# Values by key range and a larger weight pool in an attention and mixture-of-experts kernel

## The chip, the cores and the metric

The program runs on one core of a Trainium2 chip. The metric is device time in microseconds of one execution; the kernel before was run three times. Besides, one execution was taken by the hardware profiler; all rows come from that one.

## What is computed

The inputs are q, k, v of 4 batches, 8 heads, 576 positions and 64 dimensions in float32. Two attentions are added: one over queries, keys and values averaged over groups of 4 positions (144 of them), whose result is repeated 4 times, and one over the 576 positions in which a query sees only keys nearer than 4 positions. The sum is laid out as 2304 tokens of 512 numbers. A router takes, from the token times `w_gate` plus noise scaled by a second product, the two best of 8 experts. Each chosen expert computes `relu(x @ w1[e]) @ w2[e]` with 1024 hidden numbers, and the two results are added with softmax weights.

```
out_d = sm_attn(q_d, k_d, v_d)              # means over 4 positions
out_up = np.repeat(out_d, 4, axis=2)
mask = np.abs(pos[:, None] - pos[None, :]) < 4
out_local = np.matmul(softmax(where(mask, scores, -1e9)), v)
x = (out_up + out_local)                    # 2304 x 512
noisy_logits = x @ w_gate + log1p(exp(x @ w_noise)) * noise
out[mask] += top2_w * (relu(x[mask] @ w1[e]) @ w2[e])
```

## The kernel before, in words

**Attention and routing.** The local attention is cut into 20 tiles n, five for each batch, of 116 queries in two halves s of 58; a half sees a window of 64 keys (`geo`, line 661). For each tile the values of both windows are loaded (`l_load_v`, 666), the scores are made in pieces of 32 queries and 38 keys (`l_qk`, 682) on top of a mask that is put there by a product with the identity (687), then maximum, exponential, sum and scaling (`l_max`, `l_exp`, `l_sum`, `l_norm`), a transpose (`l_pt`, 726), the products with the values (`l_pv`, 737), the sum with the pooled attention into `xT` (`l_x`, 761), a transpose to rows (`l_xt`, `l_xtc`) and a store to DRAM (`l_store`, 785), and the router's logits (`l_lg`, `l_lgt`, `l_ls`). Five groups of token tiles are routed (`r_...`), and each token is scattered into a list of its expert by POOL (`r_put`, 950).

In the kernel before, a value tile has for each s two half-tiles of 64 partitions, one for each parity j of the head, with head parity and key range changing places between the two s (`j ^ s`); that makes four transfers of 64 KB, each with 64 x 4 runs of 256 bytes. The scores follow the same order: the PSUM bank is `j ^ s`, and a group of 32 partitions t stands for s = t % 2.

**Who orders the work.** Up to expert 1's first products all work is a list of steps (`Step`, 273), each with an engine, an estimated time, a priority, what it must come after, and the buffers it takes and uses. `run_steps` (309) goes through them in three stages and writes the instructions out: of the steps that an engine could do, it takes the one with the earliest possible start, then the lowest priority number. The resulting order is fixed in the program; the engines run it in order and wait for one another by semaphores. To each priority is added an offset from the table `OFF` (364), four numbers for each kind of step, for the four quarters of its steps. For SP the planner holds a running end of the transfers (`free["move"]`) and lets SP be at most 4 us ahead of it (`LEAD`). `light` steps need not be done at the end of stage 2; they may be taken later. `keep_warm` (431) writes fillers (products of ones, line 440) into holes of PE that it foresees, and where it counts too little work on PE; `LOAD` (464) says how many columns each kind counts for.

**Queues.** All plain loads and stores are issued by SP in the planned order: `t_load` (492, q and k), `vd_load` (549), `l_load_v` (673, with small transfers at 680 for the two tiles at the edges), `l_store` (786), the weights (`fetch_w`, 226 and 229), and six fills of the output with zeros (201, 768 KB each). POOL issues the indirect transfers: lists, gathers of tokens, reads and writes of output rows.

**Expert 0 and the others.** Stages 2 and 3 hold expert 0 (`b_gemm`, 1247, in two parts; `o_part`, 1362) and what prepares expert 1. Each weight tile of 256 KB is fetched into a `raw` buffer of the pool `stage` (three buffers), and split into two parts by ACT (236) and DVE (241). At the end of stage 2 the attention's memory is given back, and the pools for w2, gathered tokens and output rows are opened in its place. Then comes a loop over experts 1 to 7 (1621): for each of 8 column blocks f `gemm1` (1411), for each of 5 token tiles `gemm2` (1442); a fetch is written two blocks ahead of its split.

Of the kernel before, what the change touches and what calls it, by code (L numbers as in the profile page):

```python
# [22 lines left out]
def kernel(  # L23
# [113 lines left out]
    def c_masks():  # L137
        for mi in range(3):
# [73 lines left out]
    raws = {}  # L212
# [60 lines left out]
    class Step:  # L273
        def __init__(self, kind, eng, dur, fn, after=(), new=(), use=(), prio=0.0, move=0.0, light=False, lag=0.0, cols=0, stage=1, table=None):
# [34 lines left out]
    def run_steps(stage):  # L309
# [55 lines left out]
        "a_acc": (-35.8, -29.9, -41.4, 31.4), "a_count": (2.1, 21.3, 57.6, 27.6),  # L365
        "a_holes": (-13.6, -13.6, -13.6, 5.5), "a_list": (-28.2, -28.2, -28.2, -28.2),
        "a_part": (34.5, 17.5, 19.9, 17.3), "a_rows": (63.6, 53.8, 45.5, 68.8), "b_gather": (70, 40.2, 38.5, 70),
        "b_gemm": (70, 70, -1.7, 69.5), "b_hi": (-5.8, -53.4, -5.8, -11), "b_list": (3, -7.6, 32.7, 10.7),
        "b_lo": (-18.8, 26.1, 33.4, 15.7), "b_order": (-3.1, 15.9, 0.8, -53.3), "b_pe": (-23.6, 17.4, 36.4, -2.4),
        "b_relu": (-8.2, 29.4, 20.6, 20.6), "b_rest": (-44.2, -1.4, 0.1, -5), "b_rows": (-15.8, -15.8, -15.8, -15.8),  # L370
        "b_weights": (67.8, 27.4, 37.6, 70), "c_count": (-7.2, 26.4, -2.5, 24.3),
        "c_fills": (-49.8, -50.9, -49.8, -49.8), "c_first": (58.9, 58.9, 58.9, 58.9),
        "c_ids": (-24.5, -3.7, -53.2, -26), "c_masks": (-32.2, -32.2, -32.2, -32.7),
        "c_rank": (43.6, -14.4, 44.9, -11.3), "c_route": (37.4, 35.5, 35.5, 35.5), "c_sel": (36.1, 36.1, 36.1, 36.1),
        "c_tiles": (64.7, -32.5, 60.3, -8.6), "d_exp": (-34.8, -4.1, 50, 48.6), "d_max": (-33.9, -40.6, -31.6, -12.5),
        "d_norm": (-2.9, -28.4, 23.9, -56.6), "d_pt": (7.3, -56.4, -42.1, -22.2), "d_ptc": (53.7, -56.9, -48.7, 21.1),
        "d_pv": (-41, -62.6, -1.1, -6.4), "d_qk": (-38.9, -36.4, -70, 7.8), "d_rz": (-28.1, 38.2, 2.2, 41.2),
        "d_up": (-16.3, 11.3, 13, 23.2), "e_go": (33.5, 40.3, 40.2, 40.3), "e_hi": (13.3, 13.3, 13.3, 11.3),
        "e_lo": (70, 43.8, 66, 70), "e_order": (-0.7, 38.7, 6.6, 25.9), "e_pe": (13.8, 52.4, 45.7, 34.4),
        "fetch_e": (55.6, 41.4, 55.6, 44.5), "fetch_w1": (56.2, 21.6, 43.6, 70), "fetch_w2": (7, 7, 7, 7),  # L380
        "fill_list": (-63.8, -37.3, 46.9, -59.5), "fill_out": (69, 56.5, 66.7, 66.7),
        "gather": (68.9, -37.6, 13.3, 46.3), "hi_e": (45.6, 48.8, -6.3, 59.6), "identb": (64.2, 70, 60.7, 39.3),
        "l_exp": (47.9, 57.6, 9, 32.8), "l_lg": (5, 4, -47.3, -36.8), "l_lgc": (-23, -22.4, 11.2, 3.9),
        "l_lgt": (-19.5, -3.7, 52.2, 58.9), "l_load_v": (-1.4, 7, 18.4, 15.9), "l_ls": (-27.7, -44.1, -11.5, 61.4),
        "l_max": (42, 35.3, -9.2, 40.9), "l_norm": (-40.5, -35.4, -39.8, -38.5),
        "l_norml": (-28.7, -52.7, -53.5, -56.9), "l_pt": (2.8, 3.6, 6.5, -5.2), "l_ptc": (-3.1, 46.3, -56.1, 39.2),
        "l_pv": (12.7, -7.4, 25.3, 7.1), "l_qk": (68.4, 62.8, 45.1, 68.4), "l_store": (-51, -50.8, -23.1, -40.9),
        "l_sum": (52.7, 48.4, 66.6, 66.5), "l_x": (-43.4, -61.4, -62.6, -66.4), "l_xt": (-68.7, -18.3, -5.3, 8.4),
        "l_xtc": (49.6, 19.4, 69.8, 18.1), "list_rows": (-21.4, -21.4, -21.4, -21.4), "lo_e": (31.8, 67.7, 52.9, 47.2),
        "load_list": (50.6, 43.3, 49.1, 57.3), "load_noise": (13.3, 57, 8, 70), "load_wgn": (-25.5, -1, -51.2, 68.7),  # L390
        "masks": (-19.2, -13.1, -19.2, -19.2), "o_mul": (-28.1, -27.4, 34.8, -31.1), "o_part": (-16, 42.8, 37.7, 40.1),
        "o_put": (32.9, 5.5, -9.1, 5.5), "ones": (35.8, -24.2, -12.1, -57), "r_count": (65.3, 69.7, 61.2, 69.7),
        "r_hot": (54.2, 26.5, 59.7, 49.5), "r_oh": (-55.9, 24.4, -20.9, -53.4), "r_pay": (70, 1.5, 69.4, 68.8),
        "r_pos": (70, 70, 70, 50.3), "r_put": (-5.2, -13.1, -12.5, 9.1), "r_slot": (-28.8, 13.6, 60.5, 29.8),
        "r_soft": (-60.1, -60.1, -62.8, -60.1), "r_top": (31.8, -0.7, -39.8, 16.5), "r_wexp": (41.8, 56.1, 54.8, 52.9),
        "r_where": (9.4, 3.3, 5, -29.5), "sp_zero": (47.1, 47.1, 49, 47.4), "split_hi1": (14.2, 5.5, 32.8, 14.2),
        "split_hi2": (46.9, 12.2, 20.3, 25.2), "split_lo1": (46.2, 0.6, 70, 70),
        "split_lo2": (34.7, 30.6, -36.3, 22.4), "t_copy": (58.7, 39.5, -16.7, 23.1),
        "t_load": (-32.5, -18, -20.5, -13.1), "t_new": (-32.4, -69.4, -37.9, 23.9), "t_pe": (-39.8, 51.4, 54.6, 67.6),
        "t_sum": (-57.2, -29.3, -19, -19), "t_sumq": (40.8, 45, 34.7, 48.9), "vd_load": (-1.5, -3.6, -1.9, 9.1),  # L400
        "vd_sum": (-27.8, -4.2, -3.3, -4.2), "vd_sum2": (70, 70, 69.8, 70), "vd_zero": (-70, -44.5, -48.7, 55.6),
        "warm": (-18.5, -7.9, 20, -7.4), "which": (65.1, 66, 60.4, 65.1)}
# [9 lines left out]
    def buf(name, early=False):  # L412
        return Buf(R[name], early or name in EARLY)
# [17 lines left out]
    def keep_warm(t, t1):  # L431
# [23 lines left out]
        while t1 > 8.0 and sum(w for e, w in warm[-64:] if e > t1 - WARM_T) < WARM_C:  # L455
# [8 lines left out]
    LOAD = {"t_pe": 1024, "l_qk": 1536, "l_pt": 1024, "l_pv": 512, "l_xt": 1024, "l_lg": 512, "l_ls": 64, "d_qk": 576,  # L464
            "d_pt": 1024, "d_pv": 864, "b_pe": 1024, "e_pe": 1024}
# [200 lines left out]
    def l_load_v(n):  # L666
        b, i, t0, ws = geo(n)
        st["vw", n] = vw = wk.tile([P, 2, NP, D], F32, tag="vw", name=f"vw{n}", bufs=R["vw"].bufs)
        for s in range(2):
            for j in range(2):  # L670
                row = (b * H + (j ^ s)) * S + ws[s]
                a0, a1 = int(row < 0), NP - int(row + 2 * (NP - 1) * S + 64 > B * H * S)
                nc.sync.dma_start(
                    out=vw[64 * j : 64 * j + 64, s, a0:a1],
                    in_=bass.AP(v.tensor, v.offset + (row + 2 * a0 * S) * D, [[D, 64], [2 * S * D, a1 - a0], [1, D]]))
                lo, hi = max(ws[s], 0), min(ws[s] + 64, S)
                for a in {*range(NP)} - {*range(a0, a1)}:
                    for p0, k0, w in ((lo - ws[s], lo, hi - lo), (0, 0, lo - ws[s]), (hi - ws[s], hi - EDGE, ws[s] + 64 - hi)):
                        if w:
                            nc.sync.dma_start(out=vw[64 * j + p0 : 64 * j + p0 + w, s, a], in_=v[b, (j ^ s) + 2 * a, k0 : k0 + w, :])  # L680
# [56 lines left out]
    def l_pv(n):  # L737
# [3 lines left out]
        for pr in range(NP):  # L741
            for s in range(2):
                for j in range(2):
# [17 lines left out]
    def l_x(n):  # L761
        b, i, t0, ws = geo(n)
        o = st.pop(("o", n))
        for k, g, c, w in pieces(n):
            if g == 0:
                st["xT", k] = xo.tile([P, NP, P], F32, tag="xT", name=f"xT{k}", bufs=R["xT"].bufs)
# [912 lines left out]
```

## Time and profile before

| | us |
|---|---|
| median of 3 runs | 637.38 |
| lowest and highest | 635.91, 638.97 |
| profiled execution, its own time | 643.82 |
| span of the profiled execution | 642.1 |
| PE busy in the span | 596.8 (93%) |
| DVE busy in the span | 403.6 (63%) |

The span goes from the first to the last instruction; the execution's own time has a little more around it. Busy time of an engine is a sum over its instructions; register, semaphore and transfer-issuing instructions don't count, so SP, which only issues, shows up in its queue's timeline and not here. The share of the whole span says little, since the stages have different limits.

### The profile page before, as it was taken

Reading aid. Unit: us, or ns where it says so; the run is one execution under the profiler, and the core shown is the slowest. Engines: PE = TensorE matmul, PEld = TensorE weight load, DVE = VectorE, ACT = ScalarE, POOL = GpSimd, SP = SyncE. Lnnn points to the kernel's source line nnn. Section 1 sums busy time; section 2 is a strip of 40 time slices with the busy share of each in tenths; the row PEclk is TensorE's granted clock in tenths of the full one; section 3 lists DMA queues with packets and bytes.
Section 4 is the critical chain, followed back from the end, with each engine's and each line's share of the span. In section 5 each row is a group of like instructions: output and inputs, shape, how many; then the busy total and the mean of one; then the engine's idle time right before and its main releaser. Section 6 shows DMA issues by size and latency. Waiting matters only on the chain. (4 is left out here: it accounts for less than half of the span.)

```text
span 642.1 us, 15186 instructions
## 1 busy us (share of the span) xinstructions
PE 596.8 (93%) x5748; PEld 517.9 (81%) x5748; DVE 403.6 (63%) x1099; ACT 316.0 (49%) x758; POOL 232.3 (36%) x319
## 2 busy tenths in 40 slices
PE   7879999687779989999999999999999999999995
PEld 7667777556669879998898799889789879888975
DVE  4776888578347746477458638736766775784521
ACT  3546687335335324366357528616645753763400
POOL 7462645647432714222233233323223133222111
PEclk9887999768669999999999999999999999999998
DMA  9984976568722846454354445345445455443401
GB/s 172 193 171 100 226 147 181 109 161 212 220 51 85 143 103 197 144 149 150 122 165 129 147 157 156 124 132 172 126 154 157 122 159 173 134 154 109 126 20 49
DMA packets 129206, 91.54 MB, mean 143 GB/s; under 512 B 72115, under 2 KB 109491, under 8 KB 129124
## 3 DMA queue, kind: packets, MB, share of 16 engines
q1 hardware_dynamic: 119172, 62.72, 39.2%
q0 software_dynamic: 9952, 27.77, 14.2%
q8 instruction: 46, 0.75, 0.5%
q14 instruction: 36, 0.29, 0.2%
HBM read 71.38 MB, written 19.38 MB: 141 GB/s over the span
## 5 line engine op out<-in xcount | busy, mean ns | idle before, releaser
L1461 PE MATMUL py<-w1h,h 128*128 128x512 f32 (+4 forms) x544 | 169.2, 389 | 0.6 <-DVE ga L1469 0.6
L1420 PE MATMUL ph<-xh,w0h 128*128 128x288 f32 (+3 forms) x448 | 133.9, 299 | 0.6 <-PEq L1583 0.4
L1420 PE MATMUL ph<-xh,w0l 128*128 128x288 f32 (+3 forms) x448 | 133.7, 298 | 0.0
L1420 PE MATMUL ph<-xl,w0h 128*128 128x288 f32 (+3 forms) x448 | 133.6, 298 | 0.0
L1461 PEld LDWEIGHTS py<-w1h,h 128*128 128x128 f32 (+3 forms) x544 | 99.3, 186 | 26.5 <-ACT w1h L236 1.2
L1461 PE MATMUL py<-w1l,h 128*128 128x512 f32 (+5 forms) x288 | 111.3, 389 | 0.0
L1429 ACT ACTIVATE h<-ph 128x512 fp32r<-128x512 f32 (+3 forms) x88 | 42.7, 485 | 112.3 <-PE ph L1420 82.8
L1470 POOL DMA_INDIRECT out_dram<-ga,lt x35 | 37.8, 1081 | 155.2 <-DVE ga L1469 112.6
L1430 DVE SCALAR_TENSOR_TENSOR h<-ph,h 128x512 fp32r<-128x512 f32 (+3 forms) x88 | 48.1, 546 | 63.4 <-ACT h L1429 54.9
L1420 PEld LDWEIGHTS ph<-xh,w0h 128*128 128x128 f32 x448 | 84.4, 188 | 2.0 <-issue 0.9
L1420 PEld LDWEIGHTS ph<-xl,w0h 128*128 128x128 f32 x448 | 84.5, 189 | 0.3
L1420 PEld LDWEIGHTS ph<-xh,w0l 128*128 128x128 f32 x448 | 84.4, 188 | 0.0
L1336 ACT ACTIVATE xr<-tr 32x128 f32<-32x128 f32 x220 | 68.1, 310 | 3.1
L1461 PEld LDWEIGHTS py<-w1l,h 128*128 128x128 f32 (+4 forms) x288 | 51.7, 180 | 14.2 <-DVE w1l L241 1.3
L1437 POOL DMA_INDIRECT ga<-out_dram,cl x35 | 34.7, 993 | 73.1 <-PE ph L1420 51.5
L236 ACT ACTIVATE w0h<-raw 128x512 fp32r<-128x512 f32 x64 | 39.0, 626 | 35.9 <-DMA raw<-in_moe_w_dram 35.4
L1469 DVE SCALAR_TENSOR_TENSOR ga<-py,lt,ga 128x512 f32<-128x512 f32 (+4 forms) x32 | 23.5, 733 | 50.0 <-PE py L1461 49.9
L241 DVE TENSOR_TENSOR w1l<-raw,w1h 128x512 fp32r<-128x512 f32 x64 | 44.2, 691 | 16.7 <-ACT w1h L236 11.9
L1208 POOL DMA_INDIRECT gx<-x_d,cl x35 | 36.7, 1048 | 45.8 <-PE ph L1420 27.2
L1338 DVE COPY xr<-tr 32x128 f32<-32x128 f32 x220 | 50.5, 229 | 2.8
L953 POOL DMA_INDIRECT list_d<-pay,sli x36 | 36.6, 1016 | 30.9 <-DVE h L1271 22.2
L236 ACT ACTIVATE w1h<-raw 128x512 fp32r<-128x512 f32 x64 | 40.2, 628 | 13.0 <-DMA raw<-in_moe_w_dram 8.5
(208 smaller groups left out, 1001.6 us busy)
## 6 DMA issues: line engine op xcount, KB each, us to landing
raw<-in_moe_w_dram SPq DMA_DIRECT2D x128, 256.0 KB
vw<-in_v_dram SPq DMA_DIRECT2D x78, 64.0 KB
x_d<-x SPq DMA_DIRECT2D x18, 256.0 KB
out_dram<-zero SPq DMA_DIRECT2D x6, 768.0 KB
nat<-in_q_dram SPq DMA_DIRECT2D x16, 256.0 KB
nat<-in_k_dram SPq DMA_DIRECT2D x16, 256.0 KB
vg<-in_v_dram SPq DMA_DIRECT2D x8, 320.0 KB
vg<-in_v_dram SPq DMA_DIRECT2D x8, 256.0 KB
```

What stands on the lines that cost most here:

```text
L236: nc.scalar.activation(hi, raw, AF.Copy)
L241: nc.vector.tensor_tensor(lo, raws.pop((e, z, f)), hi.bitcast(F32), op=ALU.subtract)
L953: ins = nc.gpsimd.indirect_dma_start(out=list_d[:, :], out_offset=bass.IndirectOffsetOnAxis(ap=sli[:, kk, i : i + 1], axis=0), in_=pay[:, ...
L1208: ins = nc.gpsimd.indirect_dma_start(out=gx[: got(e, t)], out_offset=None, in_=x_rows[:, :], in_offset=bass.IndirectOffsetOnAxis(ap=lists[ ...
L1336: nc.scalar.activation(dst, src, AF.Copy)
L1338: nc.vector.tensor_copy(dst, src)
L1420: last_mm[0] = nc.tensor.matmul(ph[:, n, 0:nh], lhsT=w[:, c, :], rhs=xx[:, c, sl], start=(c == 0 and z == 0), stop=(c == NDC - 1 and z == 2))
L1429: nc.scalar.activation(hh, src, AF.Relu)
L1430: nc.vector.scalar_tensor_tensor(out=hl, in0=src, scalar=0.0, in1=hh.bitcast(F32), op0=ALU.max, op1=ALU.subtract)
L1437: after_pe(nc.gpsimd.indirect_dma_start(out=acc[: tok(e, t)], out_offset=None, in_=out[:, :], in_offset=bass.IndirectOffsetOnAxis(ap=cl[: ...
L1461: last_mm[0] = nc.tensor.matmul(py[:rows, js], lhsT=hx, rhs=w[:, js], start=(f == 0 and z == 0), stop=(f == NFC - 1 and z == len(terms) - 1))
L1470: nc.gpsimd.indirect_dma_start(out=out[:, :], out_offset=bass.IndirectOffsetOnAxis(ap=lt[:m, t, 0:1], axis=0), in_=acc[:m], in_offset=None ...
```

## The change

Value tiles now have the key range s on the partition halves, for all 8 heads: two transfers of 64 x 8 runs each. Scores and products follow: the PSUM bank is s, and a group of 32 partitions t stands for head parity t % 2. The masks for the first and the last tile cover 64 partitions, and are chosen for each s. The tiles `x`, `xT` and `lgT` move from the pool `xo`, which lasts, to the attention's pool `wk`, so their steps must be done in stage 2. A pool `late` of seven weight buffers is opened after stage 2; all later fetches use it. The table of offsets is a new one, and three numbers of `LOAD` and the planner's time for `l_load_v` are changed.

```diff
-                block = mt[0:QT, :] if mi == 1 else mt[P - QT :, :]
+                block = mt[0 : P // 2, :] if mi == 1 else mt[P // 2 :, :]
...
     def fetch_w(e, z, f):
+        late_p = late[0]
         if z == 0:
-            raw = stage.tile([P, NDC, P], F32, tag="raw", name="raw1")
+            raw = (stage, late_p)[late_p is not None and (e, z) != (0, 0)].tile([P, NDC, P], F32, tag="raw", name="raw1")
...
-            raw = stage.tile([P, DM], F32, tag="raw", name="raw2")
+            raw = late_p.tile([P, DM], F32, tag="raw", name="raw2")
...
-                if h.ring is R["scl"]:
+                if h.ring in (R["scl"], R["x"], R["xT"], R["lgT"]):
                     self.light = False
...
-        "fetch_e": (55.6, 41.4, 55.6, 44.5), "fetch_w1": (56.2, 21.6, 43.6, 70), "fetch_w2": (7, 7, 7, 7),
-        "fill_list": (-63.8, -37.3, 46.9, -59.5), "fill_out": (69, 56.5, 66.7, 66.7),
...
+        "fill_out": (54.2, 48.5, 57.6, 56),
...
-    LOAD = {"t_pe": 1024, "l_qk": 1536, "l_pt": 1024, "l_pv": 512, "l_xt": 1024, "l_lg": 512, "l_ls": 64, "d_qk": 576,
-            "d_pt": 1024, "d_pv": 864, "b_pe": 1024, "e_pe": 1024}
+    LOAD = {"t_pe": 1024, "l_qk": 912, "l_pt": 1024, "l_pv": 1024, "l_xt": 1024, "l_lg": 512, "l_ls": 64, "d_qk": 576,
+            "d_pt": 1024, "d_pv": 720, "b_pe": 1024, "e_pe": 1024}
...
     def l_load_v(n):
-        st["vw", n] = vw = wk.tile([P, 2, NP, D], F32, tag="vw", name=f"vw{n}", bufs=R["vw"].bufs)
+        st["vw", n] = vw = wk.tile([P, H, D], F32, tag="vw", name=f"vw{n}", bufs=R["vw"].bufs)
         for s in range(2):
-            for j in range(2):
-                row = (b * H + (j ^ s)) * S + ws[s]
-                a0, a1 = int(row < 0), NP - int(row + 2 * (NP - 1) * S + 64 > B * H * S)
-                nc.sync.dma_start(
-                    out=vw[64 * j : 64 * j + 64, s, a0:a1],
-                    in_=bass.AP(v.tensor, v.offset + (row + 2 * a0 * S) * D, [[D, 64], [2 * S * D, a1 - a0], [1, D]]))
...
+            row = b * H * S + ws[s]
+            a0, a1 = int(row < 0), H - int(row + (H - 1) * S + 64 > B * H * S)
+            nc.sync.dma_start(
+                out=vw[64 * s : 64 * s + 64, a0:a1],
+                in_=bass.AP(v.tensor, v.offset + (row + a0 * S) * D, [[D, 64], [S * D, a1 - a0], [1, D]]))
...
     def l_qk(n):
...
-            for t in range(4):
-                s, q0 = t % 2, QT * (t // 2)
-                for j in range(2):
+            for s in range(2):
+                for t in range(4):
+                    j, q0 = t % 2, QT * (t // 2)
...
-                        sc[QT * t : QT * t + QT, j ^ s, KT * pr : KT * pr + KT],
+                        sc[QT * t : QT * t + QT, s, KT * pr : KT * pr + KT],
...
     def l_pv(n):
-            for s in range(2):
-                for j in range(2):
-                    js, to = slice(64 * j, 64 * j + 64), slice(64 * (j ^ s), 64 * (j ^ s) + 64)
-                    mark[0] = nc.tensor.matmul(o[to, s, pr].rearrange("p (h q) -> p h q", h=2), lhsT=vw[js, s, pr],
-                                     rhs=pT[js, pr].rearrange("p (h s q) -> p s h q", h=2, s=2)[:, s], start=True, stop=True)
+            for j in range(2):
+                for s in range(2):
+                    ks = slice(64 * s, 64 * s + 64)
+                    mark[0] = nc.tensor.matmul(o[64 * j : 64 * j + 64, s, pr].rearrange("p (h q) -> p h q", h=2), lhsT=vw[ks, 2 * pr + j],
+                                     rhs=pT[ks, pr].rearrange("p (h j q) -> p j h q", h=2, j=2)[:, j], start=True, stop=True)
...
-            lv = Step("l_load_v", "sp", 2.7 + 1.1 * (n in (0, NB * B - 1)), lambda n=n: l_load_v(n), new=[vwb], prio=n - KV, move=1.5)
+            lv = Step("l_load_v", "sp", 1.5 + 1.1 * (n in (0, NB * B - 1)), lambda n=n: l_load_v(n), new=[vwb], prio=n - KV, move=1.5)
...
-    R.update({"gx": Ring(3), "ga": Ring(6)})
+    R.update({"gx": Ring(3), "ga": Ring(6), "late": Ring(7)})
...
-        rb = buf("raw")
+        rb = buf("late")
...
+    late[0] = ectx.enter_context(tc.tile_pool(name="late", bufs=7, reuse_waits="tile"))
```

## Rows read from the trace of the kernel before

**Rows 1.** The page: the span, and the granted clock in 40 slices.

```profile
span 642.1 us, 15186 instructions
...
PEclk9887999768669999999999999999999999999998
```

**Rows 2.** Stretches: us; busy PE, PEld, DVE, ACT, POOL (instructions); granted clock; DMA share; GB/s.

```profile
0.00:45.00 45.00, 34.30 (x851) 30.04 (x852) 28.97 (x80) 21.88 (x56) 29.16 (x76) 0.96 0.99 185
45.00:60.00 15.00, 14.78 (x233) 12.15 (x233) 8.10 (x25) 8.50 (x31) 1.42 (x3) 0.68 0.45 92
60.00:115.00 55.00, 49.81 (x1167) 40.52 (x1165) 47.75 (x169) 39.50 (x99) 32.54 (x43) 1.00 0.76 176
115.00:150.00 35.00, 27.34 (x500) 20.11 (x495) 22.50 (x65) 12.24 (x39) 19.70 (x31) 0.61 0.67 163
150.00:199.00 49.00, 37.02 (x470) 30.97 (x468) 26.16 (x118) 20.59 (x44) 19.52 (x33) 0.72 0.55 130
199.00:245.00 46.00, 43.81 (x270) 38.54 (x270) 29.41 (x101) 17.51 (x34) 19.66 (x30) 1.00 0.56 115
245.00:600.00 355.00, 354.37 (x2073) 314.94 (x2072) 229.65 (x527) 190.28 (x448) 103.53 (x99) 1.00 0.48 149
600.00:642.00 42.00, 35.39 (x205) 30.64 (x203) 11.08 (x19) 5.50 (x13) 6.75 (x7) 0.96 0.15 49
```

**Rows 3.** PE's timeline, 118 to 123 us: start, us, instruction, [idle before, what ended it].

```profile
119.05 0.33 PE L745 MATMUL o<-pT,vw 64*64 64x64 f32 x2 [0.70 <-DMA vw<-in_v_dram]
121.93 1.11 PE L745 MATMUL o<-pT,vw 64*64 64x64 f32 x26 [2.56 <-DMA vw<-in_v_dram]
```

**Rows 4.** Waits, 115 to 126 us: total us, times, longest.

```profile
DVE xT L767 <- PE o L745: 6.7, 1, 6.7
```

**Rows 5.** SP's queue in order of time: start, us from issue to issue, transfers.

```profile
110.44 5.24 SPq L673 DMA_DIRECT2D vw<-in_v_dram  x8
115.77 2.47 SPq L786 DMA_DIRECT2D x_d<-x  x1
...
118.81 10.63 SPq L673 DMA_DIRECT2D vw<-in_v_dram  x12
```

**Rows 6.** Waits, 170 to 180 us.

```profile
ACT pT L735 <- remote: 7.4, 1, 7.4
...
PE o L440 <- issue: 5.4, 1, 5.4
```

**Rows 7.** SP's issues by line: ns of one (min/median/max), first and last start.

```profile
L673 SPq DMA_DIRECT2D vw<-in_v_dram x80: 595/615/2609, 31.7 to 160.1; - x80
...
L492 SPq DMA_DIRECT2D nat<-in_q_dram x16: 377/590/1823, 0.8 to 75.5; - x16
...
L229 SPq DMA_DIRECT2D raw<-in_moe_w_dram x64: 327/333/957, 208.0 to 602.4; - x64
```

**Rows 8.** Busy time of line 440's fillers on PE, 150 to 199 us.

```profile
150.00:199.00 49.00, 12.91 (x125) 0.72 0.55 130
```

**Rows 9.** SP's queue, the last zero fills.

```profile
161.43 4.40 SPq L201 DMA_DIRECT2D out_dram<-zero  x3
```

**Rows 10.** PE's timeline at full clock: l_qk, l_pv and what follows each.

```profile
61.81 0.77 PE L694 MATMUL scl<-kT,qT 64*32 64x38 f32 x64
62.51 0.66 PE L503 MATMUL pt<-ident,nat 128*128 128x128 f32 x4
...
66.20 0.69 PE L745 MATMUL o<-pT,vw 64*64 64x64 f32 x32
66.83 0.66 PE L730 MATMUL ptl<-ident,sp 128*128 128x128 f32 x4
```

**Rows 11.** SP's queue, the w2 fetches of expert 0.

```profile
208.03 16.69 SPq L229 DMA_DIRECT2D raw<-in_moe_w_dram  x8
```

**Rows 12.** ACT's timeline, the first split of a w2 tile.

```profile
212.93 0.64 ACT L236 ACTIVATE w1h<-raw 128x512 fp32r<-128x512 f32 x1 [2.40 <-DMA raw<-in_moe_w_dram]
```

**Rows 13.** PE's timeline, the first product of expert 0.

```profile
198.79 0.42 PE L1256 MATMUL ph0a<-xh,w0h 128*128 128x378 f32 x1
```

More of the change, by code (lines that the diff above doesn't have):

```diff
@@ L210 @@
     wpools = [wpool, None]
-    raws = {}
+    raws, late = {}, [None]
     which = {}
@@ L386 @@
[L386 to L395, printed above, removed]
@@ L401 @@
-        "vd_sum": (-27.8, -4.2, -3.3, -4.2), "vd_sum2": (70, 70, 69.8, 70), "vd_zero": (-70, -44.5, -48.7, 55.6),
-        "warm": (-18.5, -7.9, 20, -7.4), "which": (65.1, 66, 60.4, 65.1)}
+        "a_acc": (-65.5, 19, -34.2, -52), "a_count": (11.3, -43.9, -3.3, -37.4), "a_holes": (37.3, 47.8, 6.9, 38.6),
+        "a_list": (16.8, 58.3, 50.6, -41.4), "a_part": (69.1, 70, 70, 70), "a_rows": (21, 21, 21, 21),
+        "b_gather": (7, 7, 7, 10.1), "b_gemm": (18, 50.5, -38.3, 3.6), "b_hi": (18.6, 18.6, 29.5, 18.6),
@@ new lines @@
+        "l_lgt": (2.2, -33.5, -20.8, 22.6), "l_load_v": (8.2, 7.9, 18.2, 15.8), "l_ls": (-58, 44.3, -69.5, 4.7),
+        "l_max": (-2.3, 44.8, -65.2, 18.8), "l_norm": (-69.1, -37.6, -16.3, -60.7),
+        "l_norml": (-23.5, -64.3, -32.7, -55), "l_pt": (-43.3, -42.4, -38.5, -32.9), "l_ptc": (70, 15.3, 55.1, 16.9),
+        "l_pv": (-34.7, -29.5, 44.7, -60.8), "l_qk": (58.1, -0.6, 44.4, 69.4), "l_store": (-34.3, 18.4, -6.3, -26.6),
+        "l_sum": (70, 65.1, 65, 65.9), "l_x": (-70, -70, -70, -69.3), "l_xt": (-66.6, -62.6, -67.5, -70),
@@ new lines @@
+        "l_xtc": (-22.4, -22.5, -22.5, -22.5), "list_rows": (1.6, 13, 24.5, 28.1), "lo_e": (-61.3, 5.3, -38, 17.3),
+        "load_list": (0, 0, 0, 0), "load_noise": (14.3, -7.7, 54, -26.1), "load_wgn": (-63.1, 15.8, -50.4, 17.6),
+        "masks": (8.3, 10.8, 8.5, 32), "o_mul": (-56.5, -68.4, -47.1, 9.5), "o_part": (-55.6, -40.7, -26.6, -59.8),
+        "o_put": (-43.8, -49.8, -36.2, -60.5), "ones": (-15.3, 36.7, 43.2, 66.2), "r_count": (70, 70, 63.4, 68.2),
+        "r_hot": (-59.8, 47, -26.7, -39.7), "r_oh": (-41.2, 12.2, -36.3, -66.9), "r_pay": (70, 5, 70, -6.5),
@@ L403 @@
+        "t_load": (-45.8, -17.9, -14.6, -3.3), "t_new": (-21.5, -22.8, -24.5, 65.9), "t_pe": (-29.7, -8.5, 62.1, 61.3),
+        "t_sum": (-68.5, -49.6, -68.5, -36.6), "t_sumq": (56.9, 46.6, 46.4, 46.4), "vd_load": (-1.5, -10, -5.7, -6.5),
+        "vd_sum": (41.9, 40.9, 40.9, 48.2), "vd_sum2": (64.4, 64.4, 65.1, 63.9), "vd_zero": (0.1, 9.7, 3.2, 7.1),
+        "warm": (-32.8, -40.8, 30.5, -31.3), "which": (-25.7, -14.2, 4.6, 51.1)}
     SLACK, LEAD = 0.15, 4.0
@@ L667, in l_load_v @@
         b, i, t0, ws = geo(n)
-        st["vw", n] = vw = wk.tile([P, 2, NP, D], F32, tag="vw", name=f"vw{n}", bufs=R["vw"].bufs)
+        st["vw", n] = vw = wk.tile([P, H, D], F32, tag="vw", name=f"vw{n}", bufs=R["vw"].bufs)
         for s in range(2):
-            for j in range(2):
-                row = (b * H + (j ^ s)) * S + ws[s]
-                a0, a1 = int(row < 0), NP - int(row + 2 * (NP - 1) * S + 64 > B * H * S)
-                nc.sync.dma_start(
-                    out=vw[64 * j : 64 * j + 64, s, a0:a1],
-                    in_=bass.AP(v.tensor, v.offset + (row + 2 * a0 * S) * D, [[D, 64], [2 * S * D, a1 - a0], [1, D]]))
[L676 to L680, printed above, removed]
+            row = b * H * S + ws[s]
[3 more added lines that the diff above has]
+                in_=bass.AP(v.tensor, v.offset + (row + a0 * S) * D, [[D, 64], [S * D, a1 - a0], [1, D]]))
+            lo, hi = max(ws[s], 0), min(ws[s] + 64, S)
+            for h in {*range(H)} - {*range(a0, a1)}:
+                for p0, k0, w in ((lo - ws[s], lo, hi - lo), (0, 0, lo - ws[s]), (hi - ws[s], hi - EDGE, ws[s] + 64 - hi)):
+                    if w:
+                        nc.sync.dma_start(out=vw[64 * s + p0 : 64 * s + p0 + w, h], in_=v[b, h, k0 : k0 + w, :])
     def l_qk(n):
@@ L741, in l_pv @@
         for pr in range(NP):
-            for s in range(2):
-                for j in range(2):
-                    js, to = slice(64 * j, 64 * j + 64), slice(64 * (j ^ s), 64 * (j ^ s) + 64)
-                    mark[0] = nc.tensor.matmul(o[to, s, pr].rearrange("p (h q) -> p h q", h=2), lhsT=vw[js, s, pr],
-                                     rhs=pT[js, pr].rearrange("p (h s q) -> p s h q", h=2, s=2)[:, s], start=True, stop=True)
+            for j in range(2):
+                for s in range(2):
+                    ks = slice(64 * s, 64 * s + 64)
+                    mark[0] = nc.tensor.matmul(o[64 * j : 64 * j + 64, s, pr].rearrange("p (h q) -> p h q", h=2), lhsT=vw[ks, 2 * pr + j],
+                                     rhs=pT[ks, pr].rearrange("p (h j q) -> p j h q", h=2, j=2)[:, j], start=True, stop=True)
         st["o", n] = o
@@ L765, in l_x @@
             if g == 0:
-                st["xT", k] = xo.tile([P, NP, P], F32, tag="xT", name=f"xT{k}", bufs=R["xT"].bufs)
+                st["xT", k] = wk.tile([P, NP, P], F32, tag="xT", name=f"xT{k}", bufs=R["xT"].bufs)
             nc.vector.tensor_tensor(
@@ L779, in l_xtc @@
     def l_xtc(n):
-        x = xo.tile([P, 4, NDC, 32], F32, tag="x", name=f"x{n}", bufs=R["x"].bufs)
+        x = wk.tile([P, 4, NDC, 32], F32, tag="x", name=f"x{n}", bufs=R["x"].bufs)
         nc.scalar.activation(x.rearrange("p a c i -> p c a i"), st.pop(("ptx", n)).rearrange("p c (a i) -> p c a i", a=4), AF.Copy)
@@ L794, in l_lg @@
         st["pl", n] = pl
-        st["lgT", n] = xo.tile([P, P], F32, tag="lgT", name=f"lgT{n}", bufs=R["lgT"].bufs)
+        st["lgT", n] = wk.tile([P, P], F32, tag="lgT", name=f"lgT{n}", bufs=R["lgT"].bufs)
     def l_lgt(n):
@@ L1531 @@
     for f in range(NFC):
-        rb = buf("raw")
+        rb = buf("late")
         a1 = Step("fetch_e", "sp", 0.45, lambda f=f: fetch_w(1, 0, f), after=[s_which], new=[rb], prio=70 + f, move=1.2, stage=3)
```

48 lines of the change are left out of this document (22 added, 26 removed).

## The prediction

> **What bounds the kernel now.** I read the page first for its span and its line of granted clock [rows 1], then the table of stretches [rows 2], then, for each stretch that is not full, PE's timeline, the waits and SP's queue. The profiled execution took 643.8 us (span 642.1); the median of the runs is 637.4. I make the sum against 643.8 and take the 6.4 us between the two away at the end. What a measurement of this kernel can tell from no change is about 0.5%, some 3.2 us.
>
> The reader is to see three different kernels in the table. From 245 to 600 us PE is busy 354.4 of 355 us at full clock: TensorE is the bound, and nothing that the change does to buffers or transfers can give more than a microsecond there. From 199 to 245 it is busy 43.8 of 46. All that can be won lies before 199 us, where stretches differ. In 0 to 45 the DMA engines are the bound (share 0.99). In 60 to 115 DVE (47.8 of 55) and PE (49.8 of 55) are both nearly full. In 115 to 150 nothing is full: DVE 22.5 of 35, PE 27.3, DMA 0.67, and the granted clock has a mean of 0.61, so that most of the stretch ran at 1.2 GHz instead of 2.4. In 150 to 199 it is the same: DVE 26.2 of 49, DMA 0.55, clock 0.72.
>
> What begins the poor stretch is seen on PE: in the middle of one tile's products with the values (line 745) it stood still twice for a `vw` transfer, 0.70 and 2.56 us [rows 3], and DVE waited 6.7 us behind it [rows 4]. Two levels down stands SP: it was issuing values all the time, eight transfers in 5.24 us, an x store of 2.47 us, then twelve in 10.63 us [rows 5]. DMA was not full; the transfers were late because their issues stood in one line. After the stop the clock fell to 1.2 GHz.
>
> The stretch from 150 on has other stops: from 172 to 178 us ACT waits 7.4 us for something the trace calls remote, while PE waits 5.4 us on "issue" [rows 6]. Several engines stand at once, and no value transfer is named.
>
> **The change part by part.** Values: 80 main issues at a median of 0.615 us [rows 7] are 49.2 us of SP's time; 40 at that price are 24.6, so SP gets 24.6 us back, 1.2 a tile. Bytes and runs of 256 bytes are the same, so DMA's own work is not less. Each new transfer has twice the runs, a form the trace doesn't show. Bounds: no dearer (0.615), or twice as dear (1.23, and nothing is saved). The nearest row is the `nat` load, four times the bytes of a `vw` transfer at a median of 0.590 [rows 7]: the price does not go by size, so I take 0.615.
>
> What of it is on the path: not 0 to 45 (DMA-bound), little in 60 to 115 (DVE and PE are full), but 115 to 150. Eight issues in 5.24 us become four in about 2.6, so the transfer that PE stood still for is in the queue 2.6 us sooner, against 3.3 us of standing; the twelve behind it win more. Without the stop the clock has no reason to fall there. The ends: nothing, or the stretch shrinks from 35 us to DVE's 22.5, a gain of 12.5. I take half, **-6**, because DVE's next stop, for the load of q and k or for ACT, comes in place of this one.
>
> The new priorities redraw the order of everything before 199 us. Which order comes out is not in any row. In 150 to 199, 49 us hold 26.2 us of DVE and 37.0 of PE, of which 12.9 are fillers that only keep the clock up [rows 8]. The ends: half of the 23 us by which the stretch exceeds DVE's work goes (-11), or two more stops like the one of 5.4 us come (+11). The values have been issued by 161 us at the latest, and SP then issues three zero fills of 768 KB in 4.40 us [rows 9]; with SP ahead by some 10 us this all moves forward, but the stop at 172 has no value transfer in it. I take **-4**, less than one such stop.
>
> Products with the keys (l_qk): 64 passes take 0.70 us from their first to the next group's start, 61.81 to 62.51 [rows 10]. 64 x 38 columns at 2.4 GHz are 1.01 us one after another and 0.51 two at a time: now some overlap. After the change each neighbour lies in another row half and in another column strip, before only every second one. So 0 to -0.19 us a tile, -3.9 over 20; only the tiles of 60 to 115, about half, have PE on the path: **-1**. Products with the values: 32 passes take 0.63 us (66.20 to 66.83); 32 x 64 columns are 0.85 or 0.43. Old and new order both change row half and column half together at every second step, so nothing; ends +4.4 and -4.
>
> Third stage: eight w2 fetches are issued over 16.69 us [rows 11], each third one waiting for a buffer; free, they would take 8 x 0.333 = 2.7 us [rows 7]. ACT waits 2.40 us for the first [rows 12], but PE has only 2.2 us of holes in 199 to 245. I take **-1.5**, ends 0 and -2.2. The new pool lies in memory that the attention tiles leave; the w2 tiles may wait for x tiles that now lie there too. Cover: the first split of w2 is at 212.93 [rows 12], 14 us after the first product of expert 0 at 198.79 [rows 13]; if it were gone, +3. In the experts seven buffers let SP run ahead of the splits; the cover is PE's own work, at a DMA share of 0.48.
>
> Nothing for: the masks (the same selects on 64 partitions instead of 32), the boundary tiles (as many small transfers as before), the fillers' accounting (l_qk counts for 624 columns less, l_pv for 512 more), and x, xT and lgT being kept in stage 2 (they were done before 198.79 anyway).
>
> Sum: -6 -4 -1 -1.5 = -12.5: 631.3 of the profiled 643.8, and **625** of the median 637.4.
>
> **The rivals.** *Issue time was not the limit.* The v transfers may have been late because the rings were slow (SP's 2.47 us for one x store speaks for it), or a wide transfer costs 1.23 to issue. Then only l_qk and stage 3 remain: 637.4 - 2.5 = 635, 632 to 638. The Trainium skill, DMA: Bandwidth & Descriptors, section Issuing engines are not separate DMA queues, calls the sequencer's time to issue a transfer usually small beside the transfer; by that rule this rival would be right. The trace speaks against it here: 49.2 us of issues in SP's line, and PE waiting in a stretch with a DMA share of 0.67 [rows 2, 7]. Chance 0.17, of which 0.13 within 0.5%.
>
> *Slower: the zero fills and weight fetches fall into the loads.* A freer SP issues its low-priority transfers sooner. Three fills in a row stand just before the stop at 172 us; if the new order puts them, 768 KB each, before loads that PE waits for, the stops move into the full stretch 60 to 115, and the clock falls after each. It decides from two more stops of some 5.4 us on, with the 6 us of the values kept: 637.4 + 11 - 6 = 642; without them 648. For it: no cost in the order shows such a stop, so a search need not avoid it. Against: the fills' list prices are late still. Chance 0.20.
>
> *Much faster: the tail unwinds too.* -12.5 for 115 to 150, -11 after it, -1.5 and -1 as before: 26 less, 611. For it: no engine is full in these 84 us. Against: each tile is a chain over PE, DVE and ACT, and the last tiles have little beside them. Chance 0.13 (605 to 618).
>
> **How the numbers follow.** Forecast 0.50 (618 to 632), issue no limit 0.17, slower 0.20, much faster 0.13. Faster by over 0.5% (below 634.2): 0.50 + 0.13 + 0.04 = 0.67; within: 0.13; slower: 0.20. The likeliest case's own range is 618 to 632; the stated one is 611 to 643, which leaves out the upper half of the slower case and the lower half of the much faster one, and is made by the ends -11 and +11 of the unknown order above all.
>
> **What would show it.** Some 40 main issues on line 673's successor at about 0.6 us; no `vw` wait of over 1 us at PE; the first product of expert 0 (198.79 before) at about 188, and the distance from there to the end of the span, 443 us, shorter by 1 to 2 at most; the clock before it above 0.7 in every stretch. It is wrong if that first product stays at 195 or later, if SP's price per issue is near 1.2 us, or if the clock has as many low stretches as now, at other places.

## The result, and the profile after

The kernel after takes 632.83 us (median of 20 runs, 626.43 to 640.68), the kernel before beside it 640.5 (20 runs). The ratio is **0.9892 [0.986, 0.9925]**: faster by 1.1%, some 6.9 us, where 12.4 were forecast. 637.4 x 0.9892 is 630.5: the sign and the range held, the size did not. The ratio leaves out executions over 1.5% above the fastest of their kernel, so it is not exactly 632.83 / 640.5. In a second session (e10) it was 0.9888 [0.9841, 0.9935].

The page of the kernel after, beside [rows 1]: 10.9 us less span, and nearly as many low clock digits ahead of slice 12 as before.

```profile
span 631.2 us, 15074 instructions
...
PEclk9988998958859999999999999999999999999998
```

The stretches that stand against [rows 2], in the same columns:

```profile
60.00:115.00 55.00, 48.56 (x1130) 39.26 (x1129) 47.32 (x162) 38.26 (x96) 30.25 (x40) 0.97 0.80 182
115.00:150.00 35.00, 29.26 (x520) 22.56 (x520) 29.00 (x101) 19.17 (x54) 25.37 (x43) 0.80 1.02 207
150.00:199.00 49.00, 35.15 (x460) 30.22 (x460) 26.45 (x120) 19.10 (x39) 17.68 (x30) 0.76 0.49 140
199.00:245.00 46.00, 46.00 (x295) 41.05 (x294) 29.75 (x85) 17.06 (x35) 20.97 (x27) 1.00 0.62 145
```

The stretch 115 to 150 became what the prediction said: clock 0.80 for 0.61, DVE 29.0 us for 22.5. But 150 to 199 is as poor as it was (its last 7 us are now expert 0's; 150 to 192 has a clock of 0.72), and 199 to 245, which had 2.2 us of holes, has none. Next SP's price for a value transfer (against the first row of [rows 7]; ns of one, min/median/max, first and last start) and the first product of expert 0 [rows 13]:

```profile
L672 SPq DMA_DIRECT2D vw<-in_v_dram x40: 595/630/1604, 31.6 to 134.3; - x40
```

```profile
191.96 0.42 PE L1255 MATMUL ph0a<-xh,w0h 128*128 128x378 f32 x1
```

A transfer of twice the runs costs 0.630 for 0.615, so SP's 24 us were freed as reckoned, and the last of these transfers is issued at 134 instead of 160. The first product comes 6.8 us earlier; from there to the end of the span are 439.2 us instead of 443.3. I cut every profile there, at **the first product**: the part ahead (attention) and **the distance** behind it (experts).

Where did the poor stretch go? The waits of 165 to 180 us (total, times, longest) answer to [rows 6]:

```profile
DVE xT L766 <- remote: 10.7, 1, 10.7
ACT x L781 <- remote: 10.0, 1, 10.0
...
PE o L440 <- DVE xT L766: 6.9, 1, 6.9
```

No `vw` wait is left at PE, but DVE, ACT and PE stand together near 171 to 177, as they did from 172 to 177 before. That row names PE's wait after DVE's, and DVE's and ACT's after something that the trace does not see.

### The profile page after: what moved, and what is told of

Same layout as the page of the kernel before. It is cut to its first block, busy times and chain, and to the rows that moved or that the text cites. A ratio compares the mean times of both kernels' runs of the same rounds, so it can differ in the third digit from the quotient of the medians.

```text
span 631.2 us, 15074 instructions
## 1 busy us (share of the span) xinstructions
PE 587.6 (93%) x5711; PEld 512.8 (81%) x5711; DVE 402.9 (64%) x1099; ACT 313.0 (50%) x758; POOL 234.1 (37%) x319
## 5 line engine op out<-in xcount | busy, mean ns | idle before, releaser
L1436 POOL DMA_INDIRECT ga<-out_dram,cl x35 | 36.2, 1033 | 72.9 <-PE ph L1419 51.4
L242 DVE TENSOR_TENSOR w1l<-raw,w1h 128x512 fp32r<-128x512 f32 x64 | 43.7, 687 | 10.9 <-ACT w1h L237 10.0
L242 DVE TENSOR_TENSOR w0l<-raw,w0h 128x512 fp32r<-128x512 f32 x64 | 41.6, 684 | 0.4
```

Of the source, the lines that this page charges most:

```text
L242: nc.vector.tensor_tensor(lo, raws.pop((e, z, f)), hi.bitcast(F32), op=ALU.subtract)
L1436: after_pe(nc.gpsimd.indirect_dma_start(out=acc[: tok(e, t)], out_offset=None, in_=out[:, :], in_offset=bass.IndirectOffsetOnAxis(ap=cl[: ...
```

## The experiments

16 runs on four chips. Each ratio is to the kernel before on the same chip, whose median was 639.3 (e1 to e4), 626.6 (e5 to e8), 643.6 (e9 to e12) and 624.8 us (e13 to e16). "Together" adds up the gaps of over 0.6 us ahead of 250 us in which none of PE, DVE and ACT is busy.

| kernel | ratio [95%] | first product | distance | together |
|---|---|---|---|---|
| before, first profile | 1 | 198.8 | 443.3 | 15.2 |
| after, first profile | 0.9892 [0.986, 0.9925] | 192.0 | 439.2 | 10.3 |
| e1 two transfers, old order | 0.9989 [0.9954, 1.0024] | 191.4 | 443.3 | 10.0 |
| e2 four transfers, new order | 0.9928 [0.9881, 0.9974] | 197.8 | 439.2 | 4.0 |
| e3 old priorities | 1.0046 [1.0014, 1.0078] | 195.6 | 447.3 | 4.1 |
| e4 three late buffers | 1.0116 [1.0061, 1.0171] | 185.6 | 457.6 | 11.2 |
| e5 seven buffers alone | 0.9968 [0.9929, 1.0007] | 179.7 | 440.7 | 3.4 |
| e6 new early, old late | 0.9978 [0.994, 1.0015] | 177.1 | 444.4 | 2.2 |
| e7 old early, new late | 1.0297 [1.0237, 1.0356] | 184.9 | 455.1 | 3.8 |
| e8 fills with the last stores | 1.0006 [0.9963, 1.0049] | 184.6 | 447.9 | 6.7 |
| e9 before again | profile only | 197.7 | 444.4 | 11.6 |
| e10 after again | 0.9888 [0.9841, 0.9935] | 192.4 | 440.0 | 13.5 |
| e11 four transfers again | 0.9893 [0.9853, 0.9934] | 195.3 | 441.1 | 11.6 |
| e12 no late fillers | 0.9848 [0.9772, 0.9924] | 191.9 | 440.1 | 8.7 |
| e13 gathers behind | 0.9899 [0.9853, 0.9945] | 173.0 | 439.2 | 3.0 |
| e14 seven buffers again | 0.9965 [0.9929, 1.0001] | 179.0 | 440.5 | 2.3 |
| e15 no late fillers again | 0.9894 [0.9848, 0.994] | 181.5 | 439.9 | 2.8 |
| e16 old order, no late fillers | 0.9972 [0.9938, 1.0007] | 173.5 | 442.9 | 6.3 |

How to read it: the distance repeats to 1 or 2 us from chip to chip for a given order and number of buffers (442.9 to 444.4 for the old order with three, 439.2 to 441.1 for the new one with seven, e8 apart). The first product does not: the old order gave 198.8, 197.7, 191.4, 179.7 and 179.0. It is a chip's matter first of all, and one profile of it proves nothing; there only the ratios speak.

**The transfers alone (e1).** The kernel before with the new layout of the values, its products and masks; the planner keeps its old cost of a load, so each engine's order is that of before.

```diff
-    st["vw", n] = vw = wk.tile([P, 2, NP, D], ...)      # four transfers a tile
+    st["vw", n] = vw = wk.tile([P, H, D], ...)          # two, all heads, a key range each
     lv = Step("l_load_v", "sp", 2.7 + ...
```

> The kernel before with the value tiles by key range (two transfers a tile, masks, scores and products to match), but the planner told the old time for the step, so every engine's order is that of the kernel before. If the number of SP's issues is what the change takes away (issue theory), the 2.56 us wait of PE for vw near 119 us is gone, the first product of expert 0 comes at about 192 us instead of 198.8, and the time is about 7 us (1.1%) below the kernel before. If the new order does it (order theory), this is within 0.5% of the kernel before.

0.9989. SP's price and the table of stretches of e1:

```profile
L672 SPq DMA_DIRECT2D vw<-in_v_dram x40: 596/627/3812, 31.8 to 150.8; - x40
```

```profile
60.00:115.00 55.00, 50.49 (x1031) 40.67 (x1032) 44.68 (x156) 36.21 (x90) 29.81 (x39) 0.89 0.84 178
115.00:150.00 35.00, 26.14 (x627) 20.75 (x626) 27.85 (x89) 17.59 (x51) 22.03 (x35) 0.89 0.70 157
150.00:199.00 49.00, 37.80 (x437) 31.03 (x435) 28.32 (x134) 21.73 (x44) 17.81 (x31) 0.79 0.59 139
```

The stop for `vw` is gone, the clock of 115 to 150 rose to 0.89 and the first product came at 191.4, all as the issue theory had it, and the time did not move. The wait that I built on was real, but not what the time hung on. Nor did it come alike in each execution of the old order with four transfers. Between 60 and 200 us PE waits 0.3 us for values in e14, not at all in e5 and e16, and in e9 (total, times, longest):

```profile
PE o L745 <- DMA vw<-in_v_dram: 1.6, 3, 1.0
```

**The transfers taken back (e2, e11).** The kernel after, with each transfer cut in two by heads: 80 issues again, in the new order.

```diff
-    nc.sync.dma_start(out=vw[64 * s : 64 * s + 64, a0:a1], ...
+    for b0, b1 in ((a0, 4), (4, a1)):
+        nc.sync.dma_start(out=vw[64 * s : 64 * s + 64, b0:b1], ...
```

> The changed kernel with each value transfer cut in two again (heads 0 to 3, heads 4 to 7), every engine's order as in the changed kernel. Issue theory: SP's line is longer by 24 us again, PE waits for vw by more than 2 us in 100 to 130 us, the first product of expert 0 comes 4 to 7 us later than 192.0 and the time is within 0.5% of the kernel before. Order theory: as the changed kernel, 1.1% below the kernel before.

> The new order with each value transfer cut in two (80 issues instead of 40), now in one session with the kernel after. If the transfers are worth nothing: within 0.3% of after (their intervals overlap). If the new order needs SyncE's freed 25 us: 0.4 to 1% above after, and a later first product at the same distance of 439.

e2 gave 0.9928, when after was known from another session: between the two theories, with the first product 5.8 us later than in after but without any wait of PE for `vw`. So it was measured once more beside after: 0.9893 (e11) against 0.9888 (e10). PE's longest waits of 60 to 199 us in e11 have the `vw` stop back:

```profile
PE o L440 <- DVE xT L767: 7.9, 3, 7.0
PE scl L687 <- DVE sb L706: 3.5, 1, 3.5
PE o L745 <- DMA vw<-in_v_dram: 3.3, 2, 2.1
```

3.3 us of PE's standing for values, as much as the 3.3 that I priced at 6 us [rows 3], and no loss that can be told. In neither order does the halving show a gain; e1's interval leaves room for 0.46%, 2.9 us, and not for 6. Both orders were compared on chips of the slower kind (639 and 644 us); on the two faster ones the halving alone was not tried.

**The priorities and the buffers, each alone (e3, e4, e5, e14).** The new kernel with the old table of priorities; with the planner and the pool at three late buffers; and the kernel before with seven late buffers of which its planner is not told.

```diff
-    OFF = {"a_acc": (-65.5, 19, -34.2, -52), ...                 # e3
+    OFF = {"a_acc": (-35.8, -29.9, -41.4, 31.4), ...
-    R.update({..., "late": Ring(7)})   ...   name="late", bufs=7  # e4
+    R.update({..., "late": Ring(3)})   ...   name="late", bufs=3
+    late[0] = ectx.enter_context(tc.tile_pool(name="late", bufs=7, ...   # e5, e14
```

> The changed kernel with the old table of priority offsets; two transfers a tile, seven buffers and the planner's new times stay. Issue theory: about as the changed kernel, 0.5% to 1.1% below the kernel before, first product of expert 0 at 190 to 195 us. Order theory: the first product at 198 us or later, and only the third stage's 2 to 4 us are left, 0.3% to 0.6% below.

> The changed kernel with three weight buffers after stage 2 instead of seven, for the pool and for the planner; before the first product of expert 0 the order is the same. If the seven buffers give what was forecast, PE has 2 to 3 us of holes in the 46 us after that first product and the time from it to the end of the span is 441 to 443 us instead of 439; if they give nothing, it is 439 to 440 as in the changed kernel. The time is 0.2% to 0.6% above the changed kernel.

> The kernel before with only the pool of seven late weight buffers (and x, xT and lgT in the pool that ends with the second stage, which makes its room); the planner still reckons with three, so every engine's order is that of the kernel before. If buffers alone pay in the tail: ratio to before 0.994 to 0.997, and the first product of expert 0 to the end of the span is 439 to 441 us instead of 443.3. If seven buffers only serve an order that was planned for them: ratio 0.998 to 1.002, distance 443 +- 0.5.

> Seven late buffers alone in the old order once more. If they are worth the 2.6 us by which the distance behind the first product fell: ratio 0.995 to 0.997, distance 440 to 441.5. If not: 0.998 to 1.002.

Buffers alone: 0.9968 and 0.9965, intervals that each only just reach 1, with the distance at 440.7 and 440.5, 2.6 to 2.8 below 443.3 (and 442.9 in e16, three buffers on e14's chip). Some 2 us, for the tail that needed no new order. The new order with three buffers is the worst of both: 1.0116, some 2.2% above after where 0.2 to 0.6% were expected. Its SP queue (start, us, transfers) holds the w2 fetches up, and the planner sets filling products (`pw`) where it expects TensorE to wait:

```profile
187.17 22.37 SPq L230 DMA_DIRECT2D raw<-in_moe_w_dram  x7
```

```profile
L436 PE MATMUL pw<-ones 128*128 128x128 bf16 x136 | 9.9, 242 | 0.0
```

e3, 1.0046, is above the kernel before, where both theories had it below. The same group in e3 (count, busy us) makes up most of its longer distance:

```profile
L437 PE MATMUL pw<-ones 128*128 128x128 bf16 x98 | 6.0, 219 | 0.0
```

Its distance, 447.3, less these 6.0 is 441.3, near the 440.7 of e5. Behind the first product PE has hardly a gap (7.8 us idle of 447.3, after 7.2 of 439.2), so a filler that stands there looks paid in full; before and after have none. That is accounting: no run left these fillers out. In e4 they explain half, 457.6 - 9.9 = 447.7, with PE idle for 13.2 us.

**Half of the priorities (e6, e7).** The new table for attention's steps with the old one for the third stage's and expert 0's (kinds b_, c_, e_, o_, the late fetches and splits), and the mirror of it.

```diff
-    OFF = new table
+    OFF = {k: (old if k in third_stage_kinds else new)[k] for k in new}   # e6; e7: exchanged
```

> The kernel after with the old priorities for the steps of the third stage and of expert 0's chain (b_, c_, e_, o_, the late weight fetches and splits), the new ones for all others. If the gain after the first product comes from the third stage's new order: ratio 0.993 to 0.996, distance 442 to 447. If it comes with the attention's new order, which leaves the third stage a better start: ratio 0.988 to 0.991, distance 439 to 440.

> The mirror of it: the kernel after with the new priorities for the third stage's and expert 0's steps alone. If the third stage's order is what pays: distance 439 to 441, ratio 0.993 to 0.997, since the attention's gain is lost. If the attention's order pays: distance 443 to 448 and ratio 1.000 to 1.005, as with all old priorities (1.0046, 447.3).

Neither expectation of e7 held, nor did a sum of halves: 1.0297, with 121 `pw` fillers (7.6 us) behind the first product and 107 of the other kind (line 403 there, 440 in after; 6.3 us): 455.1 - 13.9 = 441.2. e6 has 76 (4.6 us): 444.4 - 4.6 = 439.8, which is after's distance; its ratio, 0.9978, is above both that were expected, though its interval reaches the first. Half of the table keeps little of the gain (e6) or does worse than all of the old (e7 against e3's 1.0046): a table of priorities is one piece.

**The zero fills (e8).** The six fills behind the x stores 12 to 17 instead of at 137 to 148 us.

```diff
-    Step("fill_out", "sp", 0.45, lambda f=f: fill_out(f), ...
+    Step("fill_out", "sp", 0.45, lambda f=f: None, ...
+    # in l_store(n), behind the store: fill n - 12, for n of 12 to 17
```

> The kernel after with its six zero fills issued behind the x stores 12 to 17 instead of in one burst at 137 to 148 us; all else in the same order. If the burst (DMA share above 1 from 130 to 155) starves the engines there and sets off the half clock at 130 to 140 and 170 to 190: 3 to 6 us faster than after, ratio 0.980 to 0.985, and the common stop near 171 to 177 gone. If the stop has nothing to do with the fills: ratio 0.987 to 0.991, the stop stays (4 us or more with none of TensorE, VectorE, ScalarE busy between 165 and 180). If the fills now hold up the stores and weight fetches: ratio above 0.993.

The third case: 1.0006, the whole gain lost. The profiled execution took 634.2 us against a median of 627.0, so its 447.9 is not to be set beside the others. PE's waits of 184 to 206 us, SP's queue ahead of them, and a stretch in the columns of [rows 2]:

```profile
PE ph0a L1258 <- ACT w0h L237: 4.7, 1, 4.7
```

```profile
182.27 1.19 SPq L201 DMA_DIRECT2D out_dram<-zero  x1
183.87 6.08 SPq L227 DMA_DIRECT2D raw<-in_moe_w_dram  x3
```

```profile
184.00:196.00 12.00, 7.31 (x54) 6.94 (x48) 2.96 (x19) 0.91 (x3) 0.00 (x0) 0.99 1.07 224
```

The last w1 fetches stand behind the fills while the DMA engines are full (share 1.07), and expert 0 stops for them just after it began. The burst at 137 to 148 (DMA share 1.02 in 115 to 150) costs less than the same fills at these later places.

**Before and after once more on one chip (e9, e10).**

> The kernel before, unchanged, for a profile on the chip of the next three. On this chip or another, the distance from expert 0's first product to the end of the span is 443 +- 1; the time of that first product goes with how long TensorE, VectorE and ScalarE stand still together before it (15 us of such stops and 198.8 in the first profile of it; 3.4 us and 179.7 in a run of the same order).

> The kernel after, unchanged. If its gain is 4.1 us behind the first product and some 3 us ahead of it, whatever the chip: ratio 0.986 to 0.992 also where the kernel before takes 626 us, distance 439 +- 1. If the gain was only that the new order came round a stop that the chip of the first comparison had: ratio 0.992 to 0.998 on a chip without it.

0.9888, on a chip whose kernel before takes 643.6; e9's distance, 444.4, lies 0.4 above what was expected. This chip has the stops too, so it does not tell whether the gain needs them. e13 and e15 below speak against it: after with one small change each, on a chip where they have 3.0 and 2.8 us of stops, at 0.9899 and 0.9894. The two parts of e9 and then of e10 (us; busy PE, PEld, DVE, ACT, POOL; clock; DMA share; GB/s):

```profile
0.00:197.65 197.65, 162.70 (x3206) 132.03 (x3206) 134.90 (x453) 102.42 (x265) 102.22 (x184) 0.84 0.74 159
197.65:642.10 444.45, 434.52 (x2547) 385.53 (x2544) 269.23 (x647) 212.53 (x494) 131.62 (x135) 0.99 0.47 135
```

```profile
0.00:192.42 192.42, 154.51 (x3166) 127.69 (x3167) 133.11 (x448) 102.13 (x265) 100.86 (x184) 0.87 0.88 168
192.42:632.40 439.98, 432.67 (x2549) 385.00 (x2546) 268.42 (x652) 210.53 (x493) 132.34 (x135) 1.00 0.46 135
```

Here the first product is 5.2 us earlier and the distance 4.5 shorter. Behind it PE is idle 9.9 us before and 7.3 after; e9's waits there show 2.1 us for `w1h`, which e10 has not. Ahead of it PE's idle time did not fall (35.0 to 37.9 us): what fell is its busy time, by 8.2 us, of which 3.6 are fillers (31.8 us to 28.2).

**The fillers ahead of expert 0 (e12, e15, e16).** After, and before, without those that the planner sets after the 110th microsecond of its own estimate; the traces hold 199 of 300 and 201 of 337.

```diff
     def put(n):
+        if not pw and t1 > 110.0:
+            return
```

> The kernel after without the filling products that the planner sets after its 110th microsecond (102 of 300; some 8 to 10 us of TensorE in the profile of after, most of them between 150 and 199); all else in the same order. If the fillers stand in front of work that is ready, as the term of -4 us for the new priorities took it: 2 to 6 us faster than after, first product earlier by as much. If they stand where TensorE waits anyway: within 0.3% of after. If they hold the clock up: slower than after, more low clock digits in slices 8 to 12.

> The kernel after without its 102 late filling products once more. If they cost what they fill: ratio 0.980 to 0.986. If they stand where TensorE waits anyway: 0.987 to 0.991, as after.

> The kernel before without its 137 filling products after the planner's 110th microsecond (13 us of TensorE between 150 and 199). If the old order loses by its fillers, as the term of -4 us took it: ratio 0.988 to 0.994. If they fill waits: 0.998 to 1.002. If they hold the clock up: above 1.002.

0.9848 (six runs, a wide interval), 0.9894 and 0.9972: e15 stands where after stands, and e16's gain, if there is one, is 0.3%. So these fillers cost nothing that can be told, unlike, by the accounting above, those behind the first product. That they stand where PE waits anyway does not follow. The stretch ahead of the first product in e12, and in e13 (all fillers, next paragraph) and e15 on one chip, beside e10's row above:

```profile
0.00:191.91 191.91, 154.01 (x3065) 125.75 (x3065) 134.88 (x445) 102.03 (x264) 101.26 (x184) 0.82 0.82 167
```

```profile
0.00:172.95 172.95, 144.64 (x3166) 119.34 (x3167) 135.08 (x448) 101.47 (x265) 100.89 (x184) 0.94 0.91 185
0.00:181.51 181.51, 154.15 (x3066) 127.21 (x3066) 132.59 (x445) 102.22 (x264) 101.02 (x184) 0.82 0.84 175
```

With 101 products fewer PE is busy as long as in e10 (154.0 us to 154.5) or longer than in e13 (154.2 to 144.6), and the granted clock is lower, 0.82 for 0.87 and 0.94: the remaining products took the time that the fillers gave up. That is the sign that the third case named, without its loss of time. In the old order it does not show (e16 0.88, e14 on the same chip 0.89). One execution of each is too little to say more.

**The early row gathers (e13).** Expert 0's first three row gathers, moved behind the five list scatters that follow them on POOL.

```diff
     def b_gather(t, n_rows=N):
+        if t < NTA: held.append((gxa[t], t, n_rows)); return
     def b_order(t):
+        while held: gather0(*held.pop(0))
```

> The kernel after with expert 0's three early row gathers moved behind the five list scatters that follow them on GpSimd (3.9 to 9 us later, still ahead of their first reader); all else in the same order. If the rows that they move make the three engines stand still (170 to 177 in after): the stop moves to 178 to 185 or goes, the first product comes 2 to 5 us earlier, ratio 0.980 to 0.986. If the stop has another cause: it stays at 168 to 178, ratio 0.987 to 0.991.

0.9899, as after. The stop is gone, but on this chip it is gone from e14 and e15 too, where nothing was moved (e16 has one of 3.6 us). The run tells nothing of its cause.

## Why the prediction was right or wrong

**"49.2 us of issues in SP's line", -6: the step that failed.** That halving the issues frees 24 us of SP is right, and that a stop for `vw` goes with them (none in after, e1 and e10; back in e11, if not in e2). The clock of 115 to 150 did rise, but in the new order it is 0.79 and 0.76 with four transfers too (e2, e11), so the halving alone does not explain it. What failed is "what of it is on the path". e1 freed all of it and gained 0.1% +- 0.35; e11 put it back and came out at 0.9893 where after has 0.9888. The 2.56 us wait ended last at that instruction in that execution. Take it away and PE comes sooner to the next thing that is late; that this is above all the stop of all three engines near 170 is a guess, no run shows it. My lower end, nothing, was the answer; I took half way to the upper one because the stop stood where the clock fell. It did, and it still did not set the time. The rival "issue time was not the limit" had the outcome of this step right, not its reasons: a wide transfer costs 0.630 us and not 1.23, and that the rings were slow was not tried. The Trainium skill (DMA: Bandwidth & Descriptors, section Issuing engines are not separate DMA queues) calls the time of an issue usually small beside its transfer; the runs agree in so far as 40 issues of 0.63 us more or less change nothing here that can be told. That rival's 635 was too high all the same, since it gave the priorities nothing.

**"-4" for the priorities** was about right in size: with seven buffers in both, 0.9888 or 0.9892 against 0.9965 or 0.9968 is 0.8%, 5 us. This sets ratios from different chips beside each other and takes in the planner's other new numbers; the other way round, the old table in the new kernel, it is 1.5% (e3). It was wrong in place: about 1 of these lies behind the first product (440.6 with the buffers alone, 439.2 to 440.0 with both), not in 150 to 199, and the 12.9 us of fillers there, which I counted as room, are none: taking them out gained nothing that can be told (e12, e15, e16). How the rest divides ahead of the first product stays open; e9 and e10 show it as PE's work done at a higher mean clock (0.84 to 0.87) with fewer fillers, in one execution of each.

**"-1.5" for the seven buffers** measured 2.1 us (0.34% of 625) alone, within my end of -2.2, and in part at the place that I named: PE's holes in the 60 us behind the first product went from 2.2 us to 1.3 (e5) and 0.7 (e14). The w2 fetches begin 3.8 us behind that product in e5, instead of 9.2, and 0.5 us behind it in after. There seven of the eight leave in 3.20 us (I gave eight 2.7; before they took 16.69, [rows 11]); only the eighth goes later, at 207:

```profile
192.45 3.20 SPq L230 DMA_DIRECT2D raw<-in_moe_w_dram  x7
```

**"-1" for products with the keys** fell: 64 passes take 0.71 us (63.27 to 63.98) against 0.70 [rows 10]. "0" for products with the values held: 64.56 to 65.19, 0.63 as before.

```profile
63.27 0.78 PE L693 MATMUL scl<-kT,qT 64*32 64x38 f32 x64
63.98 0.66 PE L503 MATMUL pt<-ident,nat 128*128 128x128 f32 x4
64.56 0.69 PE L744 MATMUL o<-pT,vw 64*64 64x64 f32 x32
65.19 0.66 PE L729 MATMUL ptl<-ident,sp 128*128 128x128 f32 x4
```

So the terms that were right in size, -4 and -1.5, make 5.5 of the 6.9 us. The signs that I had named were mixed: the price of an issue and the `vw` waits came as forecast, the first product was to come at 188 and came at 192, the distance was to shrink by 1 to 2 and shrank by 4.1, and the clock was above 0.7 in each stretch, if barely (0.71 in 45 to 60). One sign of being wrong came too: nearly as many low stretches of the clock as before, at other places. The rival "slower" is not what happened, though its mechanism exists: the new order does bunch the fills (four in 5.00 us from 143.59), at no loss that a run shows; in e8's profile PE waits 4.7 us for a w1 tile fetched behind fills.

One more error lies under the sum: I made it against one execution whose stops ahead of 199 us were 15.2 us together. The same order (with seven buffers) had 3.4 and 2.3 us of them on two other chips, where the kernel before takes 625 to 627 us instead of 639 to 644. A large part of the "poor stretch" was no property of the order at all. But the stops alone do not make the difference between the chips either: e2 and e3 had 4.0 and 4.1 us of them and first products at 197.8 and 195.6.

## What to carry to other kernels

A wait that one profile shows may be missing from the next, and it is worth its length only if nothing else is late right behind it: see it in a second execution, and undo that one wait alone, in the old order, before pricing what a redrawn order will make of it. Cut the profile at the last point where the bound engine starts to be full: what lies behind repeated here to a microsecond or two and can be read from single profiles, what lies ahead scattered by twenty and more and needs timed runs. Filling products cost nothing that could be told ahead of that point, and behind it, by the accounting, their full time, so count them first when a new order comes out slower. Priorities searched for one set of buffers did badly here in parts or with another set.

## What was not expected of the hardware

In eight of the eighteen profiles TensorE, VectorE and ScalarE stood still together for 4 to 6 us between 165 and 184 us. The stretches of such stops in after, e1 and e9:

```profile
170.75:176.80 6.05, 0.00 (x0) 0.10 (x1) 0.00 (x0) 0.00 (x0) 3.94 (x8) 0.50 0.11 28
```

```profile
165.85:170.80 4.95, 0.00 (x0) 0.00 (x0) 0.00 (x0) 0.00 (x0) 3.96 (x7) 0.99 1.06 276
```

```profile
173.60:177.60 4.00, 0.01 (x1) 0.00 (x0) 0.00 (x0) 0.00 (x0) 3.31 (x6) 0.84 0.87 182
```

Only POOL works there, on its chain of list scatters and row gathers; the DMA share is 0.11 in one and 1.06 in another, the clock low or full. The trace puts the waits down to "remote" or "issue". The two chips where before takes 625 to 627 us showed one such stop (3.6 us, e16) in eight profiles, the chips of e1 to e4 and e9 to e12 six in eight. The difference between these pairs of chips is some 15 us, more than twice the gain of the change. The cause of the stops was not found: moving the gathers could only be tried where the stop did not occur, and the scatters themselves were not moved.
